# A list over the whole of layer 1, operands of layer 2 summed in DRAM, and a split last tile, in an attention kernel with two dense layers behind it

## The chip, the core and the metric

The kernel runs on one core of one Trainium2 chip. Five engines of that core appear in the profile: PE (TensorE, matrix products; PEld are its weight loads), DVE (VectorE), ACT (ScalarE), POOL (GpSimd) and SP (SyncE, which issues the transfers here). The metric is the time of one execution on the device in microseconds, as a median over several executions.

## What is computed

Attention with 4 batches, 8 heads, 576 positions and a head size of 64; the first four heads see a plain window of 32 positions, the last four a window of 128 in which every fourth position counts. Its output, 2304 tokens of 512 values, goes through two dense layers with 2048 inner values each:

```python
x = attention(q, k, v)                       # 2304 x 512
h = x @ w_in1                                # 2304 x 2048
P = a0 + a1*h + a2*h*h + a3*h*h*h
Q = 1 + abs(b0)*abs(h) + abs(b1)*h*h
y = (P / (Q + 1e-6)) @ w_out1                # 2304 x 512
h = y @ w_in2
out = (maximum(h, 0) + alpha * minimum(h, 0)) @ w_out2
```

All of it is float32.

## The kernel before

**Tiling.** Tokens go in 6 blocks (NB) of 384 (BLK), each made of four attention units U (two plain, two dilated). The 2048 inner values go in 16 chunks (NC) of 128. Layer 1 runs over 48 pairs of chunks J (NP), eight for each block. For a pair, `inproj` (product at L645) makes two tiles `ps_h`; `rat_1` and `rat_2` (L663 to L677) compute the rational function on ACT and DVE in the tiles `ta`, `tb`, `tc`; `g_split` (L684, L685) splits the result; and two pairs later `outproj1` (L695) adds its part to four tiles `ps_y`. `ps_h` has two banks, so the products of a tile start when DVE's last reader of the tile two before (`tc`, L666) is done. A product of float32 accuracy is made of three products of a rounded high part and a low part (`xh`, `xl`; `winh`, `winl`). Only the first block works with unsplit float32 products (tiles `win`, `wout`).

**What else runs in layer 1.** Beside the pairs, the attention of the later units is computed, one unit in two pairs: scores on PE (L458, L478), exponentials on ACT (`att_exp`, L512), transposes (L549), the product with `v` (L582). Weights are converted from float64 words and split on ACT and DVE (`w_convert`, `w_split`). A block's result goes through `os` (L701) to a tensor in DRAM, `y_dram` (L702).

**Layer 2** works on two blocks at a time (SB = 3) by a scheme with seven products in place of eight (`st_pair`, products at L836). It needs sums of quarters of y: with B11, B21 (block 0, its two halves of channels) and B12, B22 (block 1), T1 = B12 - B11, T3 = B22 - B12, T2 = B22 - T1, T4 = B21 - T2. `x_load` (L739) reads the quarters from `y_dram`, `x_combine` (L760) subtracts on DVE, `x_place` (L742, L743) splits each of the seven into a rounded high part on ACT and a low part on DVE. For the first two blocks this is done in the last five pairs of layer 1, from J = NP - 5 on. `outproj2` (L714) makes the output tiles; L719 copies each to `os` on ACT and L721 stores it.

**What sets the order.** Within an engine the order is fixed when the program is built. By default a scheduler of the language sets it by its own costs. `in_order_of_need` runs ahead of that: it walks through all instructions with costs of its own (`_cost`), estimates landing times of transfers, takes at each step the ready instruction that has the longest chain of work behind it, and writes an order for each engine. Of that order only what starts before ORDERED (115 us by its reckoning) is imposed; the rest is left to the default scheduler, behind the last listed instruction of its engine.

**The start.** WARM products of zeros (L963) run on PE before data are there, then 64 filler products (L967) are free to stand between the first units' products.

## Time and profile before

| | |
|---|---|
| median of 3 runs | 887.02 us (885.96 to 888.42) |
| the profiled execution | 887.51 us, of which the span is 885.7 us |
| PE busy | 872.5 us, 99% of the span, 5746 products |
| DVE busy | 760.7 us, 86% |
| ACT busy | 613.3 us, 69% |
| POOL busy | 0.2 us, 4 instructions, no transfers |
| DMA | 92.78 MB, all from SP's queue but for 0.94 MB of instructions |

The end of a product is modelled, so a busy share of PE near 100% says that products followed one another, not that each ran at its peak; the time from the start of a product to the start of the next is the better measure. Layer 1 with the attention of later units fills the span to about 500 us, layer 2 the rest.

### The profile page before, as it was taken

The numbers are of one execution on the slowest core, as the hardware profiler recorded it, in microseconds if no ns is written. First come the engines' busy times: TensorE is split into PE (matmuls) and PEld (weight loads), VectorE is DVE, ScalarE is ACT, GpSimd is POOL, SyncE is SP. The second block draws the span as 40 slices with busy tenths as digits, with TensorE's granted clock in tenths as the row PEclk, the third lists the DMA queues.
The fourth block names the chain that finished last, engine by engine and source line by source line (L and its number), as shares of the span: only waits on it lengthen the run. The fifth ranks groups of instructions, "written<-read, shape, count | busy, mean of one in ns | idle before, by whom it ended". The sixth has DMA issues, their size and how long they took to land.

```text
span 885.7 us, 14822 instructions
## 1 busy us (share of the span) xinstructions
PE 872.5 (99%) x5746; PEld 779.0 (88%) x5746; DVE 760.7 (86%) x1199; ACT 613.3 (69%) x1253; POOL 0.2 (0%) x4
## 2 busy tenths in 40 slices
PE   9999999999999999999999999999999999999997
PEld 6555678999999999999999999898888989899896
DVE  5999999999999998988899999998986778767652
ACT  6999988788877888887677576557554456635423
POOL 0000000000000000000000000000000000000000
PEclk9999999999999999999999999999999999999999
DMA  9964212133334434440021242323320011210001
GB/s 346 407 238 176 82 57 79 38 115 140 130 109 139 173 125 148 160 149 19 20 78 42 95 131 95 119 79 119 101 85 24 27 46 60 97 47 25 1 0 72
DMA packets 32903, 92.78 MB, mean 105 GB/s; under 512 B 3905, under 2 KB 11329, under 8 KB 32833
## 3 DMA queue, kind: packets, MB, share of 16 engines
q1 hardware_dynamic: 32832, 91.83, 29.9%
q8 instruction: 45, 0.74, 0.3%
q14 instruction: 26, 0.20, 0.1%
HBM read 76.61 MB, written 15.20 MB: 104 GB/s over the span
## 4 chain that ended last, share of the span: by engine, by line
PE 57%; ACT 18%; DVE 18%; DMA 4%; issue 2%; SPq 0%; ACTq 0%
PE ps_h L836 19%; PE ps_y L714 14%; PE ps_y L695 9%; PE ps_h L645 7%; PE ps_aS L714 4%; PE ps_aP L714 3%; ACT p L512 3%; DVE tb L675 2%; DVE tc L676 2%; ACT p L532 2%; ACT tc L664 2%; ACT ta L673 2%; DVE tc L677 2%; ACT ta L674 2%; ACT ta L663 1%
## 5 line engine op out<-in xcount | busy, mean ns | idle before, releaser
L645 PE MATMUL ps_h<-xh,winh 128*128 128x384 f32 x320 | 110.4, 345 | 2.7 <-DVE tc L666 2.2
L695 PE MATMUL ps_y<-gh,wouth 128*128 128x384 f32 x320 | 108.4, 339 | 0.0
L695 PE MATMUL ps_y<-gl,wouth 128*128 128x384 f32 x320 | 107.1, 335 | 0.3 <-DVE gl L685 0.3
L695 PE MATMUL ps_y<-gh,woutl 128*128 128x384 f32 x320 | 107.2, 335 | 0.0
L645 PE MATMUL ps_h<-xh,winl 128*128 128x384 f32 x320 | 107.2, 335 | 0.0
L645 PE MATMUL ps_h<-xl,winh 128*128 128x384 f32 x320 | 107.1, 335 | 0.0
L714 PE MATMUL ps_y<-wouth,gl 128*128 128x512 f32 x192 | 74.9, 390 | 0.0
L714 PE MATMUL ps_y<-woutl,gh 128*128 128x512 f32 x192 | 74.9, 390 | 0.0
L714 PE MATMUL ps_y<-wouth,gh 128*128 128x512 f32 x192 | 74.8, 390 | 0.0
L663 ACT ACTIVATE ta<-ps_h,root 128x384 f32<-128x384 f32 x96 | 57.3, 596 | 18.7 <-PE ps_h L645 18.4
L664 ACT ACTIVATE tc<-ps_h,co 128x384 f32<-128x384 f32 x96 | 66.5, 694 | 0.0
L645 PEld LDWEIGHTS ps_h<-xh,winh 128*128 128x128 f32 x320 | 60.0, 188 | 6.9 <-DVE tc L666 3.7
L742 ACT ACTIVATE gh<-tc 128x768 fp32r<-128x768 f32 x48 | 40.3, 841 | 30.5 <-PE ps_aP L714 28.0
L695 PEld LDWEIGHTS ps_y<-gl,wouth 128*128 128x128 f32 x320 | 60.2, 188 | 0.6 <-DVE gl L685 0.6
L645 PEld LDWEIGHTS ps_h<-xl,winh 128*128 128x128 f32 x320 | 60.1, 188 | 0.3
L743 DVE TENSOR_TENSOR gl<-tc,gh 128x768 fp32r<-128x768 f32 x48 | 45.8, 954 | 16.9 <-ACT gh L742 16.7
L695 PEld LDWEIGHTS ps_y<-gh,wouth 128*128 128x128 f32 x320 | 60.2, 188 | 0.0
L742 ACT ACTIVATE st_a<-w 128x1024 fp32r<-128x1024 f32 x24 | 25.5, 1061 | 50.1 <-PE ps_h L836 41.4
L695 PEld LDWEIGHTS ps_y<-gh,woutl 128*128 128x128 f32 x320 | 60.1, 188 | 0.0
L645 PEld LDWEIGHTS ps_h<-xh,winl 128*128 128x128 f32 x320 | 60.1, 188 | 0.0
L675 DVE SCALAR_TENSOR_TENSOR tb<-tb,ta 128x768 f32<-128x768 f32 x48 | 45.8, 955 | 16.3 <-ACT ta L674 16.0
L666 DVE SCALAR_TENSOR_TENSOR tc<-tc,co,ps_h 128x384 f32<-128x384 f32 x96 | 58.1, 608 | 0.7
(197 smaller groups left out, 2317.8 us busy)
## 6 DMA issues: line engine op xcount, KB each, us to landing
w<-w_dram_in SPq DMA_DIRECT2D x24, 512.0 KB, 3.6
raw<-in_w_in_dram SPq DMA_DIRECT2D x16, 512.0 KB, 5.1
raw_inh<-in_w_out_dram SPq DMA_DIRECT2D x13, 512.0 KB, 3.8
ld_qk<-in_qk_d_dram SPq DMA_DIRECT2D x12, 512.0 KB, 5.0
ld_v<-in_v_d_dram SPq DMA_DIRECT2D x12, 512.0 KB, 4.1
ld_qk<-in_qk_p_dram SPq DMA_DIRECT2D x12, 416.0 KB, 4.2
ld_v<-in_v_p_dram SPq DMA_DIRECT2D x12, 384.0 KB, 3.4
y_dram<-os SPq DMA_DIRECT2D x24, 192.0 KB, 1.9
```

The source lines that it names most:

```text
L512: nc.scalar.activation(out=a["p"][h][:m, t * n:(t + 1) * n], in_=a["s"][h][:m, t * n:(t + 1) * n], func=AF.Exp, scale=scale, bias=a["nm"][ ...
L532: nc.scalar.activation(out=pv, in_=pv, func=AF.Copy, scale=rd[:m, t:t + 1])
L645: nc.tensor.matmul(out=hp[:, :BLK], lhsT=w, rhs=x, start=(k == 0), stop=(k == len(pairs) - 1))
L663: nc.scalar.activation(out=ta, in_=hp, func=AF.Abs, scale=root)
L664: nc.scalar.activation(out=tc_, in_=hp, func=AF.Identity, scale=co[:, 3:4], bias=co[:, 2:3])
L666: nc.vector.scalar_tensor_tensor(out=tc_, in0=tc_, scalar=co[:, 1:2], in1=hp, op0=ALU.add, op1=ALU.mult)
L675: nc.vector.scalar_tensor_tensor(out=tb, in0=tb, scalar=C1, in1=ta, op0=ALU.add, op1=ALU.mult)
L695: nc.tensor.matmul(out=yt[:, :BLK], lhsT=w[:, m * 128:(m + 1) * 128], rhs=g, start=(c == 0 and i == 0), stop=(c == NC - 1 and i == len(pai ...
L714: nc.tensor.matmul(out=yt, lhsT=g[:, tok], rhs=w, start=(first and i == 0), stop=(last and i == 2))
L742: nc.scalar.activation(out=hi, in_=t, func=AF.Copy)
L743: nc.vector.tensor_tensor(out=lo, in0=t, in1=hi.bitcast(F32), op=ALU.subtract)
L836: nc.tensor.matmul(out=hp, lhsT=u[:, ws], rhs=x[:, xs], start=(k == 0), stop=(k == 5))
```

## The change

Five things are changed.

- The order of `in_order_of_need` is imposed on every instruction written up to the end of layer 2's first step (LISTED), whatever time it gets; instructions behind that stand behind the last listed one of their engine that starts before 488 us (ORDERED). POOL is now among its engines, with its transfers reckoned like SP's. PE is reckoned at half its speed for the first 6.5 us (SLOW).
- For the first two blocks, T1 to T4 are no longer subtracted on DVE. At J = 17 the first term of each is copied from `y_dram` to a new tensor in DRAM, `sum_dram` (eight transfers, SP). At J = 18, 20 and 25 the second term of T1, T3 and T4 is loaded into a tile of tag `os`, negated on ACT and added by an accumulating transfer that POOL issues (two halves each, `t_minus`). At J = 28 two more accumulating transfers add T3 to T2 and T1 to T4.
- The low parts of B11, B21, T2, T3 and T4 of these blocks are made without DVE: ACT writes the rounded high part and then its negative, and an accumulating transfer adds the value from DRAM (`x_lows`, seven transfers). T1 and B22 are split as before.
- Eight warming products in place of ten.
- At the end, each of the last two blocks' three output tiles of a group has a buffer of its own tag (`qk`, `v`, `os`), and the very last tile is copied in two halves, one on DVE (`right`) and one on ACT, each with its own store.

A constant LAG is added and not used.

```diff
-ORDERED = 115e3
+LISTED = 1
+ORDERED = 488e3
-WARM = 10
+WARM = 8
+SLOW = 6500
...
-def in_order_of_need(tc, nc, places):
+def in_order_of_need(tc, nc, places, listed):
-        if i.engine in (Engine.PE, Engine.DVE, Engine.Activation, Engine.SP) and (i.ins or i.outs)
+        if i.engine in (Engine.PE, Engine.DVE, Engine.Activation, Engine.SP, Engine.Pool) and any(_is_access(a) for a in i.outs)
+    first = {id(i) for i in nc.cur_bb.bb.instructions[:listed]}
-    fixed = {Engine.PE: None, Engine.SP: None}
+    fixed = {Engine.PE: None, Engine.SP: None, Engine.Pool: None}
...
         start = max(free[e], ready_at[k])
-        if start < ORDERED:
+        if id(todo[k]) in first:
             order[e].append(k)
-        free[e] = start + costs[k][0]
-        if e == Engine.SP:
+            if start < ORDERED:
+                last[e] = k
+        pace = 2 if e == Engine.PE and start < SLOW else 1
+        free[e] = start + pace * costs[k][0]
+        if e in (Engine.SP, Engine.Pool):
             parts, width = size[k]
             begin = max(start + 1600, landed)
             landed = begin + parts * width / (412 if parts == 128 else 210)
             done = landed + (2700 if begin > start + 1700 else 900)
         else:
-            done = start + costs[k][1]
+            done = start + costs[k][1] + (pace - 1) * costs[k][0]
...
-        rest = [(k, ks[-1]) for k in range(n) if todo[k].engine == e and k not in chosen]
+        rest = [(k, last[e]) for k in range(n) if e in last and todo[k].engine == e and k not in chosen]
...
         if last:
-            os_ = ldp.tile([128, 2 * DM], F32, tag=("qk", "v")[t % 2], name="os")[:, :DM] if n >= NB - 2 else ldp.tile(
+            os_ = ldp.tile([128, 2 * DM], F32, tag=("qk", "v")[t], name="os")[:, :DM] if n >= NB - 2 and t < 2 else ldp.tile(
                 [128, DM], F32, tag="os", name="os"
             )
-            nc.scalar.activation(out=os_, in_=yt, func=AF.Copy)
             r0 = n * BLK + t * 128
-            nc.sync.dma_start(out=out[r0:r0 + 128, :], in_=os_)
+            if n == NB - 1 and t == 2:
+                os_ = os_[:, :DM // 2]
+                right = ap_.tile([128, BLK], F32, tag="pts", name="right", bufs=2)[:, :DM // 2]
+                nc.vector.tensor_copy(out=right, in_=yt[:, DM // 2:])
+                nc.scalar.activation(out=os_, in_=yt[:, :DM // 2], func=AF.Copy)
+                nc.sync.dma_start(out=out[r0:r0 + 128, DM // 2:], in_=right)
+                nc.sync.dma_start(out=out[r0:r0 + 128, :DM // 2], in_=os_)
+            else:
+                nc.scalar.activation(out=os_, in_=yt, func=AF.Copy)
+                nc.sync.dma_start(out=out[r0:r0 + 128, :], in_=os_)
...
+    Y_OF = {"B11": (0, 0), "B21": (0, 1), "B12": (1, 0), "B22": (1, 1)}
+    sum_dram = {name: dp.tile([128, 2 * DM], F32, name=f"sum_dram{name}")[:, :2 * BLK] for name in ("T1", "T2", "T3", "T4")}
+
+    def t_begin(name, first):
+
+        for i in range(2):
+            b, j = Y_OF[first]
+            nc.sync.dma_start(out=half(sum_dram[name], i), in_=y_dram[b, 2 * j + i])
+
+    def t_minus(name, second):
+
+        for i in range(2):
+            t = ldp.tile([128, DM], F32, tag="os", name="neg")[:, :BLK]
+            b, j = Y_OF[second]
+            nc.sync.dma_start(out=t, in_=y_dram[b, 2 * j + i])
+            nc.scalar.activation(out=t, in_=t, func=AF.Copy, scale=-1.0)
+            nc.gpsimd.dma_start(out=half(sum_dram[name], i), in_=t, accum_op=ALU.add)
+
+    def t_plus(name, second):
+        nc.gpsimd.dma_start(out=sum_dram[name], in_=sum_dram[second], accum_op=ALU.add)
+
+    def x_of_dram(name):
+        if name in sum_dram:
+            return [sum_dram[name]]
+        b, j = Y_OF[name]
+        return [y_dram[b, 2 * j + i] for i in range(2)]
+
+    def x_first(name):
+
+        x_alloc(0, name)
+        hi, lo = st_x[0, name]
+        parts = x_of_dram(name)
+        w = 2 * BLK // len(parts)
+        for i, t in enumerate(parts):
+            nc.sync.dma_start(out=lo[:, i * w:(i + 1) * w].bitcast(F32), in_=t)
+        st_s.setdefault(0, {})[name] = lo.bitcast(F32)
+
+    def x_lows(name):
+
+        hi, lo = st_x[0, name]
+        parts = x_of_dram(name)
+        w = 2 * BLK // len(parts)
+        nc.scalar.activation(out=hi, in_=lo.bitcast(F32), func=AF.Copy)
+        nc.scalar.activation(out=lo, in_=hi.bitcast(F32), func=AF.Copy, scale=-1.0)
+        for i, t in enumerate(parts):
+            nc.gpsimd.dma_start(out=lo[:, i * w:(i + 1) * w], in_=t, accum_op=ALU.add)
+
     def x_load(n):
-        st = st_s[n] = {}
+        st = st_s.setdefault(n, {})
         if n == 0:
-            for name in ("B11", "B21"):
-                x_alloc(n, name)
-                st[name] = st_x[n, name][1].bitcast(F32)
+            for name in ("B11", "T2", "B21", "T3", "T4"):
+                x_first(name)
+            for name, tag in (("T1", "qk"), ("B22", "v")):
+                st[name] = stage("st_" + name)
+                for i in range(2):
+                    src = half(sum_dram["T1"], i) if name == "T1" else y_dram[1, 2 + i]
+                    nc.sync.dma_start(out=half(st[name], i), in_=src)
+            return
         else:
             st["B11"] = st["T2"] = wp.tile([128, 2 * BLK], F32, tag=SPARE[0], name="st_b11")
             st["B21"] = wp.tile([128, 2 * BLK], F32, tag=SPARE[1], name="st_b21")...
         assert J < NP - 5 or not early
         if J == NP - 5:
             x_load(0)
+        step = {18: (t_minus, "T1", "B11"), 20: (t_minus, "T3", "B12"), 25: (t_minus, "T4", "B22")}.get(J)
+        if J == 17:
+            for name, first in (("T1", "B12"), ("T3", "B22"), ("T4", "B21"), ("T2", "B11")):
+                t_begin(name, first)
+        if step:
+            step[0](*step[1:])
+        if J == 28:
+            t_plus("T2", "T3")
+            t_plus("T4", "T1")
         if J == NP - 4:
-            x_combine(0)
-            x_place(0, "T2")
+            x_lows("T2")
             w_loads(2, 1)
             st_raw[0] = st_wload(0)
         if J == NP - 3:
             w_next(2)
-            x_place(0, "B11")
-            x_place(0, "B21")
+            x_lows("B11")
+            x_lows("B21")
         if J == NP - 2:
             st_ops = {0: st_prep(0, st_raw.pop(0))}
-            x_place(0, "T3")
-            x_place(0, "T4")
+            x_lows("T3")
+            x_lows("T4")
             st_raw[1] = st_wload(1)
     x_place(0, "T1")
@@ -1094,6 +1170,8 @@
     for n in range(SB):
         for q in range(NQ):
             k = n * NQ + q
+            if k == LISTED:
+                listed = len(nc.cur_bb.bb.instructions)
             def before():
                 if rest:
```

## Rows read from the trace of the kernel before

**Rows 1.** Busy time by stretch: window, length, PE, PEld, DVE, ACT, POOL, clock, DMA share, GB/s
```profile
60.00:80.00 20.00, 20.00 (x104) 11.65 (x106) 19.20 (x34) 20.00 (x49) 0.00 (x0) 1.00 0.72 264
...
220.00:320.00 100.00, 98.80 (x830) 95.52 (x829) 91.79 (x149) 83.04 (x212) 0.00 (x0) 1.00 0.41 139
...
440.00:500.00 60.00, 60.00 (x348) 60.00 (x347) 58.19 (x80) 43.56 (x64) 0.00 (x0) 1.00 0.21 71
```

**Rows 2.** Waits of PE, 115 to 440 us: total us, times, longest us
```profile
PE ps_h L645 <- DVE tc L666: 2.2, 4, 0.8
PE ps_h L645 <- DVE xl L615: 0.5, 1, 0.5
PE ps_h L582 <- ACT wouth L416: 0.4, 1, 0.4
PE ps_y L695 <- DVE gl L685: 0.3, 1, 0.3
```

**Rows 3.** Waits of PE, 440 to 886 us
```profile
PE ps_h L836 <- ACT v L871: 0.4, 1, 0.4
PE ps_h L836 <- DVE u L866: 0.3, 1, 0.3
```

**Rows 4.** Order of time around 235 us: start, us, engine, line [idle before <- releaser]
```profile
232.47 0.71 ACT L664 ACTIVATE tc<-ps_h,co 128x384 f32<-128x384 f32 x1
...
232.64 0.17 DVE L522 TENSOR_SCALAR sm<-sm 112x8 f32<-112x8 f32 x1 [1.19 <-ACT p L512]
...
234.02 0.33 PE L695 MATMUL ps_y<-gl,wouth 128*128 128x384 f32 x1
...
234.19 0.34 PE L695 MATMUL ps_y<-gh,woutl 128*128 128x384 f32 x1
...
234.61 0.61 DVE L666 SCALAR_TENSOR_TENSOR tc<-tc,co,ps_h 128x384 f32<-128x384 f32 x1
...
235.28 0.45 PE L645 MATMUL ps_h<-xh,winh 128*128 128x384 f32 x1 [0.75 <-DVE tc L666]
```

**Rows 5.** Line L760, DVE: duration ns min/median/max, first and last start
```profile
L760 DVE TENSOR_TENSOR st_T<-st_B,st_T x3: 947/948/949, 408.9 to 638.6; 128x768 f32<-128x768 f32 x3
```

**Rows 6.** Groups by line on ACT, 120 to 500 us: count | busy us, mean ns
```profile
L701 ACT ACTIVATE os<-ps_y 128x384 f32<-128x384 f32 x20 | 9.9, 513 | 0.8 <-PE ps_y L695 0.6 <-DMA y_dram<-os 0.2
...
L742 ACT ACTIVATE st_T2h<-st_t 128x768 fp32r<-128x768 f32 x1 | 0.8, 837 | 0.0
```

**Rows 7.** Transfers by line: count, KB each, median us to landing
```profile
ld_qk<-in_qk_p_dram SPq DMA_DIRECT2D x12, 416.0 KB, 4.2
...
raw_inh<-in_w_in_dram SPq DMA_DIRECT2D x8, 512.0 KB, 9.7
...
st_T<-y_dram SPq DMA_DIRECT2D x6, 192.0 KB, 3.0
```

**Rows 8.** Tile `st_T4h`: duration ns min/median/max, first and last start
```profile
L836 PE MATMUL ps_h<-st_T4h,st_a x96: 334/334/426, 506.3 to 860.4; 128*128 128x384 f32 x96
...
L743 DVE TENSOR_TENSOR st_T4l<-st_T,st_T4h x3: 946/948/948, 481.7 to 740.4; 128x768 fp32r<-128x768 f32 x3
```

**Rows 9.** Line L963, the warming products: duration ns, first and last start
```profile
L963 PE MATMUL ps_h<-warm x10: 379/634/634, 1.3 to 4.8; 128*128 128x512 bf16 x10
```

**Rows 10.** Order of time on SP and PE, 0.9 to 5.5 us
```profile
1.17 0.42 SPq L439 DMA_DIRECT2D ld_qk<-in_qk_p_dram  x1
...
5.36 0.37 PE L478 MATMUL ps_y<-ld_qk 64*64 64x96 f32 x5
```

**Rows 11.** Order of time at the end
```profile
880.79 0.39 PE L714 MATMUL ps_aP<-woutl,gh 128*128 128x512 f32 x1
881.03 0.59 ACT L719 ACTIVATE os<-ps_y 128x512 f32<-128x512 f32 x1
...
881.95 0.60 ACT L719 ACTIVATE os<-ps_aP 128x512 f32<-128x512 f32 x1 [0.33 <-DMA out_dram<-os]
```

**Rows 12.** Order of time on DVE, 12 to 13 us
```profile
12.15 0.55 DVE L570 COPY pts<-ps_y 96x384 f32<-96x384 f32 x1 [0.76 <-PE ps_y L549]
```

**Rows 13.** Line L721, the output's stores: duration ns on SP's queue
```profile
L721 SPq DMA_DIRECT2D out_dram<-os x18: 332/333/338, 636.9 to 882.6; - x18
```

More of the change, by code (lines that the diff above doesn't have):

```diff
@@ L32 @@
 NARROW = 2.1
+LAG = 2700
 SLACK = 100.0
 FILL = 256
-ORDERED = 115e3
+LISTED = 1
+ORDERED = 488e3
 SIGNED = (('out', 4), ('out', 6), ('out', 8), ('out', 10), ('out', 12))
-WARM = 10
+WARM = 8
+SLOW = 6500
 ORDER = "cqiqpvqvqvvwwwwwwqvwwwwwwwwqv"
@@ L158, in in_order_of_need @@
             if fixed[i.engine] is not None:
-                (behind if i.engine == Engine.SP else soft)[k].add(fixed[i.engine])
+                (soft if i.engine == Engine.PE else behind)[k].add(fixed[i.engine])
             fixed[i.engine] = k
@@ L162, in in_order_of_need @@
         writes = [_region(a, places) for a in i.outs if _is_access(a)]
-        if i.engine == Engine.SP:
+        if i.engine in (Engine.SP, Engine.Pool):
             size[k] = writes[0][2] - writes[0][1], (writes[0][4] - writes[0][3])
@@ L210, in in_order_of_need @@
     for k in reversed(range(n)):
-        own = costs[k][1] if todo[k].engine != Engine.SP else 2500 + size[k][0] * size[k][1] / 400
+        own = costs[k][1] if todo[k].engine not in (Engine.SP, Engine.Pool) else 2500 + size[k][0] * size[k][1] / 400
         step = costs[k][0]
@@ L220, in in_order_of_need @@
     ready_at = [0.0] * n
-    free = {Engine.PE: 1300.0, Engine.DVE: 800.0, Engine.Activation: 1500.0, Engine.SP: 730.0}
+    free = {Engine.PE: 1300.0, Engine.DVE: 800.0, Engine.Activation: 1500.0, Engine.SP: 730.0, Engine.Pool: 1300.0}
     waiting = {e: [] for e in free}
@@ L226, in in_order_of_need @@
     order = {e: [] for e in free}
+    last = {}
     landed = 0.0
@@ L256, in in_order_of_need @@
     for e, ks in order.items():
+        if not ks:
+            continue
         chosen = set(ks)
-        rest = [(k, ks[-1]) for k in range(n) if todo[k].engine == e and k not in chosen]
+        rest = [(k, last[e]) for k in range(n) if e in last and todo[k].engine == e and k not in chosen]
         for b, a in [*zip(ks[1:], ks), *rest]:
@@ L786, in x_combine @@
         st = st_s[n]
-        if n == 0:
-            st["T2"] = rawp.tile([128, 2 * DM], F32, tag="u", name="st_t2", bufs=1)[:, :2 * BLK]
         sub(st["T1"], st["T3"], st["B11"])
@@ L1122, in attn_rational_prelu_kernel @@
     out_some(len(todo))
-    in_order_of_need(tc, nc, slots)
+    in_order_of_need(tc, nc, slots, listed)
 def _consts():
```

## The prediction

> **What bounds the kernel now.** I read the stretches of the span first, then who made TensorE wait, then the order of time around the longest of those waits, then the single rows of the operations that the change touches. The reader is to see that TensorE (PE) has next to nothing to wait for after the first 115 us: in layer 1 between 220 and 320 us it is busy 98.80 of 100 us, from 440 to 500 us it is busy 60.00 of 60 [rows 1]. What it does wait for between 115 and 440 us is seven waits, 3.4 us by the view (2.2 + 0.5 + 0.4 + 0.3) [rows 2], and behind 440 us two of 0.7 us together [rows 3]. So the kernel is bound by PE's own products, and the change, which takes away no product of a layer, can win only such waits, the first 115 us and the tail behind the last product.
>
> The longest wait is one of order. Around 235 us the last product of the pair starts at 234.19 and the next at 235.28, where products follow one another every 0.17 us (PE 234.02 to 234.19) [rows 4]. It waits for DVE's `tc` L666 to give back a `ps_h` bank. DVE had stood idle 1.19 us just before (until 232.64), because ACT's softmax of an attention unit stood ahead of the `tc` L664 that L666 needs; ACT came to L664 at 232.47 [rows 4]. Nothing was too slow in sum: the engines' queues were in the wrong order. Waits on `tc` L666 make 2.2 of the 3.4 us [rows 2].
>
> **The list over layer 1.** It fixes the order of PE, DVE, ACT, SP and POOL by the planner's own costs for all that is written up to the first step of layer 2 (some 500 us), in place of the first 115 us. What can go: the view counts a wait from the modelled end of a product, so the step is longer than its row: 235.28 - 234.19 - 0.17 = 0.92 us for a wait shown as 0.75 [rows 4]. Seven waits are thus 3.4 + 7 x 0.17 = 4.6 us. What speaks for the list: a stretch that it already rules, 60 to 80 us, has PE busy 20.00 of 20 although DVE is busy 19.20 and ACT 20.00 [rows 1]. That is weak proof, since there PE works on the slow products of the first block and leaves the others more time. And a planner that is off by a tenth of a microsecond makes new waits of its own. I take three quarters: -3.4 us. Bounds: -4.6 (all) and +1.5 (none won, and a third of them once more in new waits). What is late next, where these waits go, is DVE, 91.79 of 100 us busy [rows 1]; it has room, but no more than 8%.
>
> **Layer 2's first operands summed in DRAM.** Removed from DVE: four subtractions and five low parts of 768 columns, 9 x 0.95 = 8.6 us [rows 5, 8]. Added on ACT: six negations of 384 columns at 0.51 and five negated copies of 768 columns at 0.84, 3.1 + 4.2 = 7.3 us [rows 6]. On DVE the 8.6 us lie between 409 [rows 5] and 500 us, where PE waits for nothing from 440 on (60.00 of 60 [rows 1]), so they are worth 0 at once; what they leave is slack, and PE has no use for it there. ACT's 4.2 us fall where it is busy 43.56 of 60 us; its 3.1 us fall in pairs 18 to 25 of layer 1, some 70 us, where it is busy 83.04 of 100 [rows 1], so 11.9 of the 70 us are free. Cost 0 while that cover holds; if it is gone, see the second rival.
>
> The transfers: eight copies DRAM to DRAM and six loads on SP, and on POOL's queue, unused before, 15 accumulating transfers (6 + 2 + 7). The trace of before shows no accumulating one. The nearest rows are a plain read of 192 KB, 3.0 us from issue to landing, and the longest median landing of any tile, 9.7 us for 512 KB in the crowded first stage [rows 7]. What hides it: the last operand's (`T4`) low part was ready at 481.7 + 0.95 us and its first product ran at 506.3 [rows 8], 23.6 us later. With ACT's second copy (0.84) and 9.7 us in place of DVE's 0.95 it would still be 14 us early. So 0, with +0 to +2 as the bounds if SP, which waits in order, holds back a load behind a store's landing. On SP the new copies stand behind the stores of block 1 (a 192 KB transfer lands in 2 to 3 us) and ahead of the attention loads of later units, which are asked for some 20 us before they are used.
>
> **Eight warming products.** Two products fewer, at 0.38 us each by their shorter row; the first ones take 0.63 [rows 9]. The scores behind them start at 5.36 us, and the first `ld_qk`, issued at 1.17, lands about 4.2 us later, at 5.37 [rows 7, 10]: they wait for data, not for the warming. What comes after waits for the first weights, whose loads take 9.7 us [rows 7], and 64 filler products stand between. So 0; bounds -0.8 (both products, if the data were there first) and +0.5 (two products' 0.25 us that the lower level costs, 0.63 - 0.38, passed on to the scores).
> One and the same product at 0.63 and then 0.38 us is the 1.2 GHz level and then the 2.4 GHz level, with nothing but these products between. The Trainium skill (TensorE: Matmul & The Clock Gate, "What's actually happening") says that the throttled state is the default and activity releases it; by that rule, fewer products could leave the scores and the 64 filler products behind them at the lower level. This trace agrees as far as the ten products go. By the rule the sum would gain at most the +0.5 above, since what follows is hidden by loads.
>
> **The last tile.** Before: PE's last product starts at 880.79 and ends at 881.18; ACT is then in the copy of another tile (881.03 to 881.62, itself late, because its buffer is the one of the block before), and the last copy waits 0.33 us more for that buffer's store and runs 881.95 to 882.55 [rows 11]. After: three buffers per block, so both earlier copies are done when the last product ends; the last tile starts at about 881.20. One half of 256 columns on ACT: 0.60 for 512 and 0.51 for 384 [rows 11, 6] make about 0.42; on DVE 0.55 for 384 columns and 0.95 for 768 make about 0.42 [rows 12, 5]. Both end at 881.62; SP issues the second transfer 0.33 us behind the first [rows 13], at 881.95, against 882.55 before: -0.6 us. Bounds -0.9 (half the bytes land sooner) and -0.2 (the halves' copies behind one another).
>
> **The sum.** -3.4 + 0 + 0 - 0.6 = -4.0 us. The profiled execution took 887.51 us (span 885.7 and 1.8 around it), so 883.5; it stands 0.49 above the median of 887.02, so the median of the changed kernel is forecast at **883.0 us**. The forecast's own range: 881.5 (all seven waits and -0.9 at the tail) to 884.5 (half of them and -0.2). Anything within 0.3% (2.7 us: 884.4 to 889.7) is about what a measurement cannot tell from no change.
>
> **Rivals.**
> *The list only moves the waits.* PE's order comes out the same, but DVE and ACT have so little room that new waits of the same total appear elsewhere, or the waits at the block's end are in the nature of the unit (16 exponentials on ACT must go somewhere). For it: DVE at 91.79 of 100 and ACT at 83.04 [rows 1]. Against it: in rows 4 DVE stood idle for 1.19 us while PE was about to need it. Then only the tail stays: 887.0 - 0.6 = 886.4. With half won, 884.7. Chance 0.28 for the two.
> *Slower: ACT stands behind the negations' loads.* ACT's queue is now a fixed list, and each of the six negations needs a load that SP issues only when a buffer of tag `os` is free. If the planner believes the load landed and it has not, all of ACT stands: the `ta` and `tc` copies that free PE's `ps_h` banks are behind it. Price: six waits of at most one landing, 6 x 3.0 = 18 us [rows 7], of which ACT's free 11.9 us [rows 1] swallow two thirds; 6.1 us go to PE. With half of the old waits won (-2.3) and the tail (-0.6): 887.0 + 6.1 - 2.9 = 890.2. It decides from 2.0 us per negation on (11.9 / 6). Against it: the planner reckons a load longer than the 3.0 us shown (1.6 us to begin, then its bytes, then 0.9 to 2.7 us). Chance 0.12, with any time from 888 up.
> *More than forecast.* The list also re-orders the first 115 us and the stretch behind 440 us: all seven waits (-4.6), the tail (-0.9) and the two waits behind 440 us (0.7 + 2 x 0.17 = 1.0) give 880.5. Chance 0.12.
>
> **How the numbers follow.** Forecast 0.48, the rivals 0.28, 0.12 and 0.12. Range for 8 in 10: 880.5, the gain of the last case, to 887.6, which takes in "only the tail" and part of a small loss. Faster by over 0.3% (below 884.4): five sixths of the forecast (0.40), the last case (0.12) and a part of "half won" (0.08): 0.60. Slower: 0.10, most of the second rival. Same: 0.30.
>
> **What would show it.** List: in the waits of PE between 115 and 440 us, under 1.2 us in all, with no wait on `tc` L666 over 0.3 us; the exponentials of a unit broken up by `tc` copies on ACT. Operands: no first product of layer 2 waiting for a DMA; POOL's queue in the DMA table; DVE some 8 us less busy between 400 and 500 us. Tail: two copies side by side right behind the last product, and under 4.0 us from there to the end (4.5 before: 885.7 - 881.2). Wrong if PE's waits in layer 1 come to 3 us or more, if ACT's negations show idle time behind a DMA, or if the first product on `T2` or `T4` comes late.

## The result, and the profile after

The changed kernel takes 893.12 us (median of 9 runs, 890.83 to 895.64) beside 887.44 us of the kernel before (9 runs, 885.96 to 890.99): ratio 1.0061, 95% interval 1.0042 to 1.0080. It is 5.7 us slower, where 4.0 us less were forecast. (The profiles of `list_spfree` and of `sp_written` fell on executions far slower than the others, so no row is taken from them; without these executions their medians, given below as recorded, are 881.2 and 932.1 us.) Lines stand lower in the changed file: L645, L695, L836 of before are L655, L705, L904; L356, L360, L702, L739 are L366, L370, L712, L757; the first blocks' y is read at L820 and L843 in the changed kernel; the experiments' lines differ from these by a few.

A table of stages tells where. Its marks are starts of products on PE: the 65th of layer 1's `inproj` line (L645 before, L655 after), the first and the 449th of layer 2's line (L836, L904), the last product of all, and the span's end. Each column is the length of a stage in us (before), or the difference from that (all others); a row's differences add up to that of its span. Each row is one profiled execution, and each of the three stages in the middle holds the same number of products in every kernel (3228, 811 and 1109).

| kernel | span | start | layer 1 | opening of layer 2 | rest | tail |
|---|---|---|---|---|---|---|
| before | 885.70 | 66.55 | 431.45 | 160.03 | 222.76 | 4.91 |
| after | +7.98 | +3.07 | -1.25 | **+6.81** | +0.03 | -0.68 |
| list_only | +3.61 | -1.22 | -1.49 | **+6.96** | +0.04 | -0.68 |
| list_short | +5.22 | +0.93 | **+5.88** | -0.94 | +0.05 | -0.70 |
| short_dve | -0.43 | +0.06 | -0.01 | +0.13 | +0.07 | -0.68 |
| priced | +0.14 | -1.56 | -0.59 | +2.89 | +0.10 | -0.70 |
| priced40 | +9.36 | -0.15 | +7.88 | +2.29 | +0.05 | -0.71 |
| warm10 | +5.03 | +1.70 | -0.43 | +4.44 | +0.03 | -0.71 |
| sums_spfree | -3.85 | +0.06 | -3.59 | +0.33 | +0.04 | -0.69 |
| free_warm10 | -6.24 | -0.11 | -4.43 | -1.00 | -0.03 | -0.67 |
| free_slow0 | -4.96 | -0.73 | -2.74 | -0.87 | +0.06 | -0.68 |
| sp_written2 | +43.77 | +0.07 | **+43.24** | +1.12 | +0.01 | -0.67 |

The profiled execution of after, 895.45 us, is one of its slowest: its start lost 3.1 us. If the other stages are the same in the median execution, they give +4.9 (6.81 - 1.25 + 0.03 - 0.68), and 0.8 of the 5.7 us is left for the start. So one stage carries the result: the opening of layer 2.

Stretches of after (columns as in [rows 1]):

```profile
220.00:320.00 100.00, 98.91 (x828) 95.36 (x827) 85.10 (x137) 83.46 (x215) 7.17 (x8) 1.00 0.55 163
440.00:500.00 60.00, 60.00 (x348) 59.84 (x346) 53.15 (x78) 43.99 (x67) 3.41 (x4) 1.00 0.43 138
480.00:500.00 20.00, 20.00 (x117) 19.84 (x115) 16.02 (x25) 17.29 (x27) 3.41 (x4) 1.00 0.90 269
500.00:520.00 20.00, 16.91 (x91) 15.39 (x91) 16.74 (x25) 11.75 (x16) 2.85 (x4) 1.00 0.56 119
```

PE is full from 440 to 500 us, then runs 91 products in 20 us (114 in these 20 us before). DVE has 5.0 us less to do between 440 and 500 us (58.19 in [rows 1]), and PE has no use for it. The waits of PE from 115 to 440 us, against [rows 2], and, behind the dots, from 440 us on, against [rows 3] (line, releaser: total us, times, longest):

```profile
PE ps_h L655 <- DVE xl L625: 1.1, 2, 0.7
PE ps_y L705 <- ACT os L711: 0.7, 2, 0.4
...
PE ps_h L904 <- DMA st_T3l<-sum_dramT: 1.1, 1, 1.1
PE ps_h L904 <- DMA st_B21l<-y_dram: 1.0, 1, 1.0
PE ps_h L904 <- DMA st_T4l<-sum_dramT: 0.8, 1, 0.8
...
PE ps_h L904 <- DMA st_B11l<-y_dram: 0.2, 1, 0.2
```

In layer 1 the waits on `tc` are gone, and four waits of 1.8 us in all stand where seven of 3.4 stood. The exponentials of a unit are now broken up, as was expected (around 235 us a `tc` copy of ACT stands between them, at 235.17). New are the waits of layer 2's first products for the low parts that accumulating transfers bring. POOL's issues (start, length), and then two groups of the transfer table (count, KB each, median us to landing):

```profile
491.43 0.92 POOL L831 DMA_DIRECT2D st_T2l<-sum_dramT  x1 [172.62 <-ACT st_T2l L829]
492.22 1.94 POOL L831 DMA_DIRECT2D st_B11l<-y_dram  x2
499.32 0.89 POOL L831 DMA_DIRECT2D st_B21l<-y_dram  x1 [5.16 <-ACT st_s L760]
...
501.44 0.88 POOL L831 DMA_DIRECT2D st_T3l<-sum_dramT  x1
504.62 0.88 POOL L831 DMA_DIRECT2D st_T4l<-sum_dramT  x1 [2.31 <-ACT st_T1h L760]
```

```profile
sum_dramT<-neg POOLq DMA_DIRECT2D x6, 192.0 KB, 6.6
...
st_T4l<-sum_dramT POOLq DMA_DIRECT2D x1, 384.0 KB, 8.0
```

T4's low part is issued at 504.6 us and lands 8.0 us later, and PE's product that needs it starts right behind; the second line is the negated copy on ACT that the issue needs (duration, start):

```profile
512.66 0.45 PE L904 MATMUL ps_h<-st_T4l,st_a 128*128 128x384 f32 x1 [0.81 <-DMA st_T4l<-sum_dramT]
...
L829 ACT ACTIVATE st_T4l<-st_T4h x1: 849/849/849, 500.6 to 500.6; 128x768 fp32r<-128x768 f32 x1
```

Before, DVE had made that part by 482.6 us [rows 8]. No transfer here is slow beyond what was reckoned with (9.7 us of landing); the issue comes some 22 us late. T4 was read from DRAM only at 483.3 us, and then ACT's two copies of it came at 495.7 and 500.6 us by ACT's list. The queue of SP says why the reading starts so late: first before, then after (start, time in the queue, line, transfer), and last, of after, the largest of SP's waits between 380 and 520 us:

```profile
369.83 0.33 SPq L356 DMA_DIRECT2D raw<-in_w_in_dram  x1
372.97 4.90 SPq L702 DMA_DIRECT2D y_dram<-os  x4
...
389.13 0.49 SPq L360 DMA_DIRECT2D w_dram_in<-win  x1
...
447.23 4.43 SPq L702 DMA_DIRECT2D y_dram<-os  x4
452.43 0.80 SPq L739 DMA_DIRECT2D st_B21l<-y_dram  x2
```

```profile
385.84 0.90 SPq L366 DMA_DIRECT2D raw<-in_w_in_dram  x2
415.56 0.33 SPq L370 DMA_DIRECT2D w_dram_in<-win  x1
...
449.06 6.51 SPq L712 DMA_DIRECT2D y_dram<-os  x4
455.67 0.87 SPq L366 DMA_DIRECT2D raw<-in_w_in_dram  x2
477.81 0.33 SPq L370 DMA_DIRECT2D w_dram_in<-win  x1
480.44 0.80 SPq L820 DMA_DIRECT2D st_B11l<-y_dram  x2
```

```profile
SPq L370 <- DVE win L406: 79.0, 4, 28.7
```

Before, the raw words of the last of the weights that are converted ahead for layer 2 were asked for at 370 us, its conversion was stored at 389 us, and the last quarter of y for the first two blocks (B21) was read at 452 us. (The stores of y in these rows are those of blocks 3 and 4; the y of blocks 0 and 1 had been stored from 136 and 216 us on.) After, SP alternates between weights: the raw load of one stands behind the store of the one before, and that store waits for DVE's conversion. So three weights are stored at 415.6, 433.2 and 448.0 us, then come four stores of y, and the last raw load goes out at 455.7. DVE can convert only then (its last two `win` instructions run at 476.5, before at 387.8), and the reads of y stand behind this weight's store. The last line has SP standing 79.0 us for these four conversions. Two lines of the planner make that order:

```python
fixed = {Engine.PE: None, Engine.SP: None, Engine.Pool: None}
...
(soft if i.engine == Engine.PE else behind)[k].add(fixed[i.engine])
```

SP's transfers are held in the order in which the program writes them. With the list imposed for 115 us, the later transfers were left to the default scheduler; imposed for 500 us it puts each layer-2 weight's load, conversion and store into one queue with the stores and reads of y.

The tail, against [rows 11]: 4.23 us in place of 4.91, although the two copies run one after the other (ACT's half waits for DVE's; why isn't shown). The last copy now ends 1.27 us behind the last product's start (890.72 - 889.45), before 1.76 (882.55 - 880.79); the other 0.19 lie behind the copy, where the store is of half the size.

```profile
889.45 0.39 PE L724 MATMUL ps_aP<-woutl,gh 128*128 128x512 f32 x1
889.88 0.42 DVE L733 COPY right<-ps_aP 128x256 f32<-128x256 f32 x1 [6.27 <-PE ps_aP L724]
890.33 0.33 SPq L735 DMA_DIRECT2D out_dram<-right  x1
890.34 0.38 ACT L734 ACTIVATE os<-ps_aP 128x256 f32<-128x256 f32 x1 [0.54 <-DVE right L733]
```

### The profile page after: what moved, and what is told of

It is laid out like the page before. It is cut to its first block, busy times and chain, and to the rows that moved or that the text cites. A ratio compares the mean times of both kernels' runs of the same rounds, so it can differ in the third digit from the quotient of the medians.

```text
span 893.7 us, 14875 instructions
## 1 busy us (share of the span) xinstructions
PE 877.0 (98%) x5744; PEld 780.4 (87%) x5744; DVE 752.2 (84%) x1191; ACT 618.8 (69%) x1264; POOL 13.6 (2%) x19
## 4 chain that ended last, share of the span: by engine, by line
PE 69%; DVE 12%; ACT 12%; DMA 4%; issue 3%; SPq 1%; POOL 0%; DVEq 0%; POOLq 0%; ACTq 0%
PE ps_h L904 18%; PE ps_y L724 14%; PE ps_y L705 13%; PE ps_h L655 13%; PE ps_aS L724 3%; PE ps_aP L724 3%; ACT p L522 2%; PE ps_h L592 2%; ACT ta L683 2%; ACT p L542 2%; DVE tc L686 1%; ACT ta L684 1%; ACT tc L674 1%; DMA ld_qk<-in_qk_p_dram 1%; DVE tb L685 1%
## 5 line engine op out<-in xcount | busy, mean ns | idle before, releaser
L655 PE MATMUL ps_h<-xh,winh 128*128 128x384 f32 x320 | 109.7, 343 | 1.1 <-DVE xl L625 1.1
L705 PE MATMUL ps_y<-gh,wouth 128*128 128x384 f32 x320 | 108.5, 339 | 0.7 <-ACT os L711 0.7
L655 PE MATMUL ps_h<-xh,winl 128*128 128x384 f32 x320 | 107.1, 335 | 0.0
L705 PE MATMUL ps_y<-gh,woutl 128*128 128x384 f32 x320 | 107.1, 335 | 0.0
L655 PE MATMUL ps_h<-xl,winh 128*128 128x384 f32 x320 | 107.0, 334 | 0.0
L705 PE MATMUL ps_y<-gl,wouth 128*128 128x384 f32 x320 | 107.0, 334 | 0.0
L760 ACT ACTIVATE gh<-tc 128x768 fp32r<-128x768 f32 x48 | 40.4, 841 | 39.5 <-PE ps_aP L724 33.9
L760 ACT ACTIVATE st_a<-w 128x1024 fp32r<-128x1024 f32 x24 | 25.5, 1061 | 59.0 <-PE ps_h L904 38.4
L655 PEld LDWEIGHTS ps_h<-xh,winh 128*128 128x128 f32 x320 | 60.0, 188 | 4.1 <-DVE xl L625 2.0
L705 PEld LDWEIGHTS ps_y<-gh,wouth 128*128 128x128 f32 x320 | 60.2, 188 | 1.0 <-ACT os L711 1.0
L655 PEld LDWEIGHTS ps_h<-xl,winh 128*128 128x128 f32 x320 | 60.1, 188 | 0.3
L705 PEld LDWEIGHTS ps_y<-gl,wouth 128*128 128x128 f32 x320 | 60.2, 188 | 0.1
L705 PEld LDWEIGHTS ps_y<-gh,woutl 128*128 128x128 f32 x320 | 60.1, 188 | 0.0
L655 PEld LDWEIGHTS ps_h<-xh,winl 128*128 128x128 f32 x320 | 60.1, 188 | 0.0
```

Of the source, the lines that this page charges most:

```text
L655: nc.tensor.matmul(out=hp[:, :BLK], lhsT=w, rhs=x, start=(k == 0), stop=(k == len(pairs) - 1))
L705: nc.tensor.matmul(out=yt[:, :BLK], lhsT=w[:, m * 128:(m + 1) * 128], rhs=g, start=(c == 0 and i == 0), stop=(c == NC - 1 and i == len(pai ...
L760: nc.scalar.activation(out=hi, in_=t, func=AF.Copy)
```

## The experiments

Each was timed in 5 rounds beside the kernel before (`sp_written2` once). The question was whether the new way of the operands or the order is to blame, and what in the order.

**list_only**: the list, the warming and the tail kept; the operands subtracted and split on DVE as before.

```diff
...
-            x_lows("T3")
-            x_lows("T4")
+            x_place(0, "T3")
+            x_place(0, "T4")
...
```

> Operands of layer 2 subtracted and split on DVE as before; the list, eight warming products and the split last tile stay. The trace of the changed kernel has PE 1.8 us behind the kernel before at the first product of layer 2 (499.82 against 498.00) and 8.7 us behind at product 448 of L904; between them it waits for st_B21l, st_T3l and st_T4l, which accumulating transfers write. Theory A (the transfers are late): without them the 6.8 us at the border go, 893.1 - 6.8 = 886.3 us, and PE waits for no DMA between 498 and 530 us. Theory B (the list itself brings the operands late, whoever makes them): a border wait of 3 us or more stays, now behind DVE, and the time stays at 890 or more.

890.84 us against 887.39, ratio 1.0043 (1.0031 to 1.0056): theory B. The accumulating transfers are not the cause: without one of them the opening of layer 2 loses 6.96 us. The operands are as late, now on a DVE that has no idle time left (stretches, columns as in [rows 1]; then T4's low part, which ran at 481.7 us before, and the longest wait of PE there):

```profile
480.00:490.00 10.00, 10.00 (x59) 10.00 (x59) 10.00 (x15) 9.04 (x14) 0.00 (x0) 1.00 0.40 144
490.00:500.00 10.00, 8.40 (x45) 7.27 (x44) 10.00 (x16) 5.83 (x10) 0.00 (x0) 1.00 0.16 52
500.00:510.00 10.00, 8.29 (x46) 7.61 (x45) 10.00 (x14) 3.35 (x4) 0.00 (x0) 1.00 0.41 131
```

```profile
504.73 0.95 DVE L761 TENSOR_TENSOR st_T4l<-st_T,st_T4h 128x768 fp32r<-128x768 f32 x1
...
507.06 0.44 PE L901 MATMUL ps_h<-st_T4h,st_a 128*128 128x384 f32 x1 [1.71 <-DVE ta L931]
```

**list_short**: the operands' new way kept, the order imposed for 115 us only.

```diff
-ORDERED = 488e3
+ORDERED = 115e3
...
-        if id(todo[k]) in first:
-            order[e].append(k)
-            if start < ORDERED:
-                last[e] = k
+        if start < ORDERED:
+            order[e].append(k)
+            last[e] = k
```

> The list imposed only up to 115 us, as before; everything else of the change stays, the operands by accumulating transfers too. Theory A1 (the transfers take 7 to 8 us and are too slow in any order): PE still waits at the border, 4 us or more, about 891 to 895 us. Theory A2 (it is the list that starts them late: the loads of y at 480 to 485 us against 383 to 403 and later before): the loads are issued before 450 us, no wait at the border, the seven waits of layer 1 are back, about 887 us.

893.14 us, 1.0067 (1.0054 to 1.0080). The loss at the opening is gone (-0.94): it is the list's, as theory A2 had it. But layer 1 loses 5.88 us, which neither theory had. The prediction's second rival is alive here, in the default scheduler's hands: ACT stands 3.63 us for a negation's load, DVE's `xl` waits for ACT, and PE stands 1.65 us behind that:

```profile
229.59 0.52 ACT L800 ACTIVATE neg<-neg 128x384 f32<-128x384 f32 x1 [3.63 <-DMA neg<-y_dram]
...
231.14 0.44 PE L654 MATMUL ps_h<-xh,winh 128*128 128x384 f32 x1 [1.65 <-DVE xl L624]
```

This is the longest of twelve waits of PE in layer 1, 7.8 us in all; the other eleven are not traced back here.

**short_dve** takes both away: short order, operands on DVE (the edits of list_short and list_only together).

> The order imposed up to 115 us only, as in list_short (893.14 us, whose layer 1 lost 5.7 us against before), but the operands of the first two blocks subtracted and split on DVE as before: what is left of the change are the planner's other edits (PE at half speed at first, POOL among its engines), eight warming products and the split last tile. Theory R1: layer 1's loss in list_short comes from the operands' new way (negations and rounded parts on ACT, loads on SP, 15 transfers of POOL) in the hands of the default scheduler: here layer 1 loses under 1.5 us and the time is 886 to 888.5 us. Theory R2: it comes from the first 115 us as the edited planner orders them, and what follows from them: layer 1 loses 4 to 6 us here too, and the time is 890.5 to 893.5 us.

886.60 us, 0.9978 (0.9966 to 0.9991): nothing lost in layer 1 (-0.01) or at the opening, the tail's 0.68 us won: theory R1. So layer 1's loss in list_short comes from the operands' new way.

**priced** and **priced40**: in the changed kernel the planner counts 5 us more for the landing of POOL's transfers, and 15 or 40 us for one in the length of a chain.

```diff
-            done = landed + (2700 if begin > start + 1700 else 900)
+            done = landed + (2700 if begin > start + 1700 else 900) + (5000 if e == Engine.Pool else 0)
...
+        if todo[k].engine == Engine.Pool:
+            own += 15000
```

> As the changed kernel, but the planner reckons 5 us more for the landing of an accumulating transfer and 15 us more in the length of the chain behind it. Theory A2a (the planner starts them late because it reckons them at about 3 us where they take 6.5 to 8): the waits at the border fall to 2 us or less, about 887 to 888 us. Theory A2b (SP's queue, which waits in order, is held by the store of a converted weight until 478 us, and no price of the transfers changes that): loads of y again after 475 us, border as in the changed kernel, 892 to 894 us.

> As priced (889.21 us; 5 us more for the landing of POOL's transfers), but a transfer of POOL counts 40 us in the length of a chain in place of 15; SP stays in written order. Theory P: SP's queue sets when the values of y are read (467 to 475 us in priced), so a larger number moves nothing more: within 1 us of priced, 888.2 to 890.2 us, y still read behind 465 us. Theory Q: the larger number brings the reads and the accumulating transfers earlier by 10 us or more, the border's loss of 2.5 us goes under 1, and the time is 886.5 to 888 us.

priced 889.21 us, 1.0026 (1.0013 to 1.0038); priced40 896.86, 1.0101 (1.0084 to 1.0119). Dearer transfers cut the opening's loss from 6.81 to 2.89 and then only to 2.29: the reads of y, still behind the store on SP's queue, come at 467.5 and at 470.2 us (480.4 in after). priced falls between its two theories: the price moves the reads, but not out of the queue. In priced40 the reads stay where theory P had them, and the time does not. Both of its theories missed what the larger number does to layer 1: it puts the ten copies of `x_lows` on ACT nearly in one piece (475.3 to 484.4 us), five of them between the two `ta` copies of one tile; DVE waits 5.92 us for the second of these, PE stands 3.86 us, and from 487.3 us on the granted clock is 0.5 for 3.4 us:

```profile
478.39 0.92 ACT L685 ACTIVATE ta<-tb,c1t 128x768 f32<-128x768 f32 x1
...
482.15 0.83 ACT L830 ACTIVATE st_T4h<-st_T4l 128x768 fp32r<-128x768 f32 x1
482.89 0.83 ACT L686 ACTIVATE ta<-ta 128x768 f32<-128x768 f32 x1
...
483.75 0.96 DVE L687 SCALAR_TENSOR_TENSOR tb<-tb,ta 128x768 f32<-128x768 f32 x1 [5.92 <-ACT ta L686]
...
487.55 0.69 PE L657 MATMUL ps_h<-xh,winh 128*128 128x384 f32 x1 [3.86 <-DVE tc L678]
```

**list_spfree** and **sums_spfree**: list_only and the changed kernel with one edit, SP no longer held to the written order.

```diff
-    fixed = {Engine.PE: None, Engine.SP: None, Engine.Pool: None}
+    fixed = {Engine.PE: None, Engine.Pool: None}
```

> The list over layer 1 with the operands subtracted and split on DVE as before (list_only, 890.84 us, which lost 7.3 us at the border of the layers), and one thing more changed: the planner no longer holds SP's transfers in the order in which they are written, but takes them by the length of their chains like the work of the other engines. Theory P (the queue): the list nails SP to the written order, so that the last layer-2 weight's raw load stands behind a store of y (issued at 455 us), its conversion on DVE comes at 466 to 477 us in place of 380 to 388, its store at 472 to 478 us holds the loads of y behind it on the queue, and the operands of layer 2 come 20 to 70 us later than before: freed, the last weight is converted before 440 us, y is loaded before 470 us, the loss at the border is under 2 us and the time 884 to 886.5 us. Theory Q (the planner sees slack and puts off whatever is not the longest chain, whatever the queue): conversions and subtractions stay behind 460 us, the loss at the border stays 5 to 8 us, the time 889.5 to 891.5 us.

> The changed kernel with the one edit of list_spfree: SP's transfers are taken by the length of their chains. Theory P: y and the sums are read before 470 us, the accumulating transfers of the low parts are issued 10 us or more earlier than in the changed kernel (491 to 505 us), waits of layer 2's first products for their low parts fall from 4.5 us to under 1.5, and the time is 886.5 to 889.5 us. Theory Q: accumulating transfers stay at 490 to 505 us and the time at 892 to 894 us.

881.42 us, 0.9923 (0.9905 to 0.9941), and 882.05 us, 0.9936 (0.9919 to 0.9952). One edit turns 0.4% and 0.6% slower into 0.8% and 0.6% faster, more than theory P gave. Nothing but the order is changed by it, in the planner's queue of SP and so in the lists that it makes for all engines. In sums_spfree the last weight is stored at 411 us, y and the sums are read between 380 and 450 us, the accumulating transfers are issued 44 and 39 us earlier than in after, and the opening loses 0.33 us, with the same copies on ACT and the same transfers on POOL. (For list_spfree no rows are shown; free_warm10 below is the same kernel but for two warming products.) POOL in sums_spfree:

```profile
447.73 0.92 POOL L831 DMA_DIRECT2D st_T2l<-sum_dramT  x1 [127.54 <-ACT os L711]
...
465.17 0.88 POOL L831 DMA_DIRECT2D st_T4l<-sum_dramT  x1 [1.38 <-issue]
```

**sp_written**, **sp_written2**: the reverse; short_dve with SP alone held to the written order.

```diff
+    order[Engine.SP] = [k for k in range(n) if todo[k].engine == Engine.SP and id(todo[k]) in first]
+    last[Engine.SP] = order[Engine.SP][-1]
     for e, ks in order.items():
```

> The reverse of list_spfree: short_dve (886.60 us; order imposed up to 115 us, operands on DVE, no loss at the border), and one thing added: SP alone is held to the written order through layer 1, while PE, DVE, ACT keep the default scheduler's order behind 115 us. Theory P: the written order of SP is enough by itself. The last layer-2 weight's raw load then stands behind a store of y, its conversion comes behind 450 us in place of 380 to 390, the subtractions and splits of the operands pile up on DVE behind 475 us, and the border loses 4 to 8 us: 890.5 to 894.5 us. Theory L (it takes the list on DVE and ACT as well, which serves the longest chain first): under 2 us at the border, 886 to 888.5 us.

> The kernel of sp_written once more (932.68 us), for a profile of an undisturbed execution, since the first was taken in a disturbed one; it is to tell where the 46 us against short_dve are lost, ten times what theory P gave to the border. Theory P1: along layer 1, where the default scheduler's order on PE, DVE and ACT wants transfers of attention and weights earlier than the written order gives them: layer 1 loses over 30 us, in waits of PE for DVE and ACT that themselves wait for transfers, and the granted clock falls in these waits. Theory P2: at the border, over 30 us between 490 us and 560 us.

932.68 us, 1.0499 (1.0480 to 1.0517), and 931.27 the second time. The written order of SP is enough by itself to lose, but neither theory of sp_written had the place or the size: layer 1 loses 43.2 us, the opening 1.1, as theory P1 of sp_written2 has it. PE's waits from 115 to 540 us:

```profile
PE ps_y L706 <- DVE gl L696: 18.4, 7, 4.5
PE ps_h L656 <- DVE tc L677: 4.9, 7, 1.3
PE ps_y L706 <- ACT gh L695: 3.1, 3, 1.6
```

A chain from each of these waits back to a transfer is not worked out here. In this execution the granted clock also fell to 0.5 five times between 200 and 533 us, 3.4 to 6.8 us each, 27.3 us in all; at half the clock that is an estimate of 13.7 of the 43 us. With the list on the other engines as well, layer 1 loses nothing (list_only, -1.49), and the loss is at the opening of layer 2 alone. So this run shows that the queue's order matters with another order on the engines too; that the queue is the cause in the changed kernel is shown by list_spfree and sums_spfree.

**warm10** (the changed kernel), **free_warm10** (list_spfree) with ten warming products, **free_slow0** (list_spfree) without PE's half speed:

```diff
-WARM = 8
+WARM = 10
...
-SLOW = 6500
+SLOW = 0
```

> As the changed kernel with ten warming products. In the changed kernel's trace the first product of layer 1 starts at 28.01 us against 24.72, and the granted clock is 0.5 from 25.2 to 32.0 us. Theory C (two products fewer leave PE's clock to fall): granted clock 1.00 from 5 us on in this run, first product of layer 1 near 24.7 us, median 2 to 3 us below the changed kernel. Theory D (the order of the first 40 us is another, warming or not): first product of layer 1 at 26.5 us or later, median within 1 us of the changed kernel's 893.1.

> list_spfree (881.42 us) with ten warming products in place of eight. The prediction had this edit at 0 (-0.8 to +0.5). Theory W0: no difference beyond 0.8 us, 880.6 to 882.2 us. Theory W1: ten products keep PE at work longer before the first scores and the clock does not fall between 25 and 42 us in any execution: 0.8 to 2 us faster, 879.4 to 880.6 us. Either way the profile is to show, as list_spfree could not (its profiled execution was a disturbed one), the last weight converted before 440 us, y read before 470 us and no product of layer 2's first step waiting over 0.7 us.

> list_spfree (881.42 us) with PE reckoned at its full speed from the beginning (SLOW = 0), as before the change. Theory S0: the reckoning of the first 6.5 us moves little of PE's order (70 lines of some 9000), first product of layer 1 within 1 us, 880.4 to 882.4 us. Theory S1: the slow reckoning is what puts scores that wait for late loads ahead of the first products of layer 1 (25.2 to 28 us in the changed kernel's profile); without it the first product comes 1 us or more earlier, 879.4 to 880.4 us.

warm10 892.00 us, 1.0060 (1.0047 to 1.0072); free_warm10 880.25, 0.9918 (0.9905 to 0.9931); free_slow0 881.75, 0.9944 (0.9926 to 0.9962). By the medians ten products are 1.1 and 1.2 us faster than eight; beside the kernel before that was timed with each, 1.1 and 0.4 us, inside the scatter. The clock still fell for some us between 35 and 42 us in both profiles, so the reasons of theories C and W1 fail, though free_warm10's time lies in W1's range; warm10's first product of layer 1 comes at 26.31 us, a little before what theory D had. SLOW is worth nothing measurable (theory S0). Nor does either edit move only the start: in warm10 the opening loses 4.44 us, in after 6.81.

free_warm10 is the fastest version, 6.9 us below the kernel before that was timed beside it. Its queue on SP, PE's one wait between 115 and 440 us (behind 440 us there is none), and the stretch that lost 3.1 us in after:

```profile
370.87 0.33 SPq L366 DMA_DIRECT2D raw<-in_w_in_dram  x1
...
389.57 0.32 SPq L370 DMA_DIRECT2D w_dram_in<-win  x1
...
442.70 4.99 SPq L712 DMA_DIRECT2D y_dram<-os  x4
447.89 0.82 SPq L757 DMA_DIRECT2D st_B21l<-y_dram  x2
```

```profile
PE ps_h L655 <- DVE xl L625: 0.5, 1, 0.5
```

```profile
500.00:520.00 20.00, 20.00 (x112) 19.35 (x111) 18.19 (x30) 11.45 (x17) 0.00 (x0) 1.00 0.37 119
```

## Why the prediction was wrong

**The step that failed** is the 0 for the operands: "the last operand's (`T4`) low part was ready at 481.7 + 0.95 us and its first product ran at 506.3, 23.6 us later ... it would still be 14 us early". The cover, the time by which an operand is early, was read from a placement that the change itself throws away. Both numbers are the default scheduler's, and the list, counted in another term, replaces that order on DVE, ACT and SP. In after, T4's low part is asked for at 504.6 us, and the 23.6 us are no cover at all. The price inside the step was fair: 5.5 to 8.1 us of landing for accumulating transfers, under the 9.7 us taken. list_only shows that the failed step isn't about the transfers: with DVE's own 0.95 us in their place the cover is gone too. In us, the forecast of -4.0 against +5.7 is a miss of 9.7: 6.8 in the opening of layer 2, 2.1 in layer 1 (-1.25 where -3.4 stood) and 0.8 left for the start.

**The mechanism was named and mis-sized.** The bound "+0 to +2 ... if SP, which waits in order, holds back a load behind a store's landing" has the right queue. What SP waits for is not a landing of 2 to 3 us but the work in front of a store, DVE's conversion of a weight, up to 28.7 us; and the opening lost 6.8 us. Nor were the change's own copies and loads what stood in the queue: list_only has none of them.

**The list over layer 1** (-3.4; bounds -4.6 to +1.5) was right in mechanism and too large for this kernel: waits on `tc` gone, 3.4 us of waits down to 1.8 (under 1.2 was asked for), layer 1 1.25 us shorter in after and 1.49 in list_only. The size comes nearer when SP is free: -3.6, -4.4 and -2.7 us in three kernels, where all seven waits were reckoned at -4.6. The opening of layer 2 gives another 1.0 us in free_warm10, the two waits of [rows 3] of the third rival.

**Eight warming products** (0; -0.8 to +0.5): +0.4 to +1.2 in two pairs, not settled. **The last tile** (-0.6): -0.67 to -0.71 in every profile; the size is in part luck, since the copies do not run side by side (in after they end 0.49 us earlier than before, where 0.6 was reckoned).

**The rivals.** "ACT stands behind the negations' loads" gave 890.2 for slower and "any time from 888 up"; the 893.12 us lie in that range by luck, since in after ACT's six negations wait 1.6 us for loads in all, under the point from which it was said to decide (2.0 us per negation), and none of PE's four waits there comes within 15 us behind them. In list_short they wait 4.6 us in all, still under that point, and PE stands 1.65 us behind one of them: so the point was wrong too, as one wait of 3.63 us was not covered by the time that ACT has free over 70 us. "The list only moves the waits" is nearer to what happened, but the waits moved to another stage, not to other engines of the same one. (Its 884.7 for "half won" takes half of 3.4, where the range and the second rival take half of 4.6; the 0.6 us between them change nothing here.) And "what would show it" asked for DVE some 8 us less busy from 400 to 500 us: it is 0.9 less (92.52 to 91.59), since conversions that had been done by 389 us now stand there, 13.6 us of them. That line by itself points at the order.

**The sum without the queue.** With SP free the forecast of 883.0 us is missed by 1.0 us in sums_spfree, on the other side; that nearness is in part luck, since 5.9 us are won there over the kernel before that was timed beside it (887.91), where 4.0 were forecast. Two by two, medians (the kernels before beside them had 887.4 to 887.9): short order 886.60 with operands on DVE and 893.14 summed in DRAM; list as changed 890.84 and 893.12; list with SP free 881.42 and 882.05. Summing in DRAM wins in no row, and with SP free the two are within the scatter.

What stays open: the start of after. In its profile scores that wait for a load landing at 25.6 us stand ahead of layer 1's first product, the clock falls to 0.5 from 25.2 to 32.0 us, and that product comes 3.3 us later than before; the three executions with a mean clock of 0.995 or 0.996 took 894.56 to 895.64, the five at 1.0 took 890.83 to 893.12 (the ninth, at 0.999, 893.47). No run tells what makes the clock fall in some executions and not in others.

## What to carry to other kernels

Slack that is read from a trace belongs to the order that made it; when a change replaces the order, each "it is early enough" has to be worked out anew, from what its instruction will then stand behind. An order imposed on compute engines is only as good as the order of the transfer queue: let the planner place the transfers too, or look at each store in the queue that waits for work and ask which loads stand behind it. A removed load on an engine is worth nothing while another engine sets the end.

## What the hardware showed unexpectedly

In after an accumulating transfer takes 5.5 to 8.1 us from issue to landing for 192 to 384 KB (medians by tile), where SP's plain reads of 192 KB into SBUF had 3.0 before [rows 7] and 2.5 to 6.1 in after itself; POOL is held 0.87 to 1.0 us by most issues. The Trainium skill (DMA: Bandwidth & Descriptors, "Anatomy of one DMA — SWDGE (gpsimd) path") fits POOL's transfers as 2.0 us and the bytes at 436 GB/s, an estimate of 2.5 and 2.9 us for these two sizes; after's trace has more than twice that for accumulating ones, and the measurement decides. No run has a plain transfer of POOL, so what the adding itself costs is not shown.

The granted clock fell back to 0.5, the 1.2 GHz level, for 3.4 to 6.8 us between 25 and 42 us in six profiles, after 20.5 to 30.7 us at the 2.4 GHz level. In after it fell at 25.16 us, behind a wait of PE for ACT of 1.17 us that ended at 24.73. But list_short and short_dve have the same two waits of 0.43 and 0.99 us near 33 and 36 us, and the clock fell in list_short's profile (at 36.04 us) and not in short_dve's. Further on, the five falls in sp_written2 and the one in priced40 began within one of PE's longest waits there, 2.5 to 4.5 us, or in one case 0.5 us behind it (382.02 and 382.48 us).
